# A Winograd form for a 512x1536x512 matmul: seven half-block products in place of eight, in the last two batches and the tails of an attention-and-mixer kernel

## Chip, core and metric

The kernel runs on one core of a Trainium2 chip. The metric is the device time of one execution in microseconds (us). A core has five engines that run side by side: TensorE (PE in the profile; its weight loads are the row PEld), VectorE (DVE), ScalarE (ACT), GpSimd (POOL) and SyncE (SP). SBUF is the on-chip working memory, PSUM the eight banks that matmuls accumulate in.

## What is computed

A linear attention, and behind it an MLP mixer. `x` has 8 batches of 576 rows and 512 columns.

```python
def phi(x, c, s):
    r = np.maximum(x, 0.0)
    return np.concatenate([r * c, r * s], axis=-1)
...
num = np.einsum('bhsf,bhfd->bhsd', q_p, kv)
den = np.einsum('bhsf,bhf->bhs', q_p, z)[..., None] + 1e-06
x = num / den                                     # back as [batch, seq, heads * head_dim]
...
xt = x.transpose(0, 2, 1)
h = np.maximum(xt @ w_tok1, 0.0) @ w_tok2          # token mixing
u = x + h.transpose(0, 2, 1)
h2 = np.maximum(u @ w_ch1, 0.0) @ w_ch2            # channel mixing, 512 -> 1536 -> 512
return u + h2
```

The change touches only the last matmul, `... @ w_ch2`, and the addition of its result to `u`. Inputs and output are float32; the matmul operands are bf16 in the kernel and are summed in float32.

## The kernel before

A batch has 576 = 4 x 128 + 64 rows. The four full blocks of a batch go through one call of `channel`. The left-over 64 rows of all eight batches are gathered, two batches to a block of 128, in `u_tail` (four blocks); one more call of `channel`, the last thing that the kernel does, takes these tails. Batches 0 and 1 are woven by hand into one long list of operations; batches 2 to 7 and the tails go through `channel`:

```python
def channel(uT, u, store, by_slot, hooks, fine=False):
    h1 = one.tile([P, NCH, 4 * P], BF16, name="h1")
    ...
    for mi in range(NCH):                            # NCH = 12: first channel matmul
        c_ps = psM.tile([P, 512], F32, name="c_ps", tag="psM")
        for ki in range(NCC):                        # NCC = 4
            nc.tensor.matmul(c_ps, wc1[:, ki, mi * P:(mi + 1) * P], uT[:, :, ki, :], ...)
        relu(by_slot[mi], h1[:, mi, :], c_ps)        # "A": ScalarE, "D": VectorE
        step()
    for j in range(4):                               # second channel matmul
        if fine and j == 3:
            for cs in (slice(0, Dm // 2), slice(Dm // 2, Dm)):
                o_ps = psM.tile([P, Dm // 2], F32, name="o_ps", tag="psM")
                for ki in range(NCH):
                    nc.tensor.matmul(o_ps, h1[:, ki, j * P:(j + 1) * P], wc2[:, ki, cs], ...)
                nc.vector.tensor_add(u[:, j, cs], o_ps, u[:, j, cs])
                store(j, u, cs)
            break
        o_ps = psM.tile([P, Dm], F32, name="o_ps", tag="psM")
        for half in range(2):
            for ki in range(half * NCH // 2, (half + 1) * NCH // 2):
                nc.tensor.matmul(o_ps, h1[:, ki, j * P:(j + 1) * P], wc2[:, ki, :], ...)
            if half:
                nc.vector.tensor_add(u[:, j, :], o_ps, u[:, j, :])
                store(j, u)
            step()
```

`step()` issues the work of other batches that is hung on the slots of this call: while batch `p` is in `channel`, batch `p+1` goes through its attention and token mixing, and batch `p+2` has its features made. In the call for batch 6 only batch 7 is left to be hung there, in the calls for batch 7 and for the tails nothing is. Parts of batch `p+1` that matter here:

```python
def um(self, g):      # token mixing, two of the four row blocks, into PSUM
    ps = self.psum(("u", g), psA, [P, 2, Dm])
    ...
def uo(self, g):      # VectorE, 1024 elements a partition
    nc.vector.tensor_add(self.sb("u")[:, js, :], self.ps.pop(("u", g)), self.x[:, js, :])
def ubc(self, g, eng="P"):      # GpSimd makes the bf16 copy of u
    copy(eng, self.sb("ub")[:, js, :], self.u[:, js, :])
def utx(self, g):     # transposed by DMA into uT, which the next channel call reads
    nc.sync.dma_start_transpose(...)
```

PSUM is split into `psM` (four one-bank buffers, used in turn) and `psA` (two two-bank buffers). A buffer is written again only after its last reader is done. An engine works through its instructions in the order of the program. Rows go out as soon as they are added up: for a batch after every second `j`, for the tails after every `j`, and in two halves for the last one.

Of the kernel before, what the change touches and what calls it, by code (L numbers as in the profile page):

```python
# [9 lines left out]
F32 = mybir.dt.float32  # L10
BF16 = mybir.dt.bfloat16
AF = mybir.ActivationFunctionType
ALU = mybir.AluOpType

WARM = 20
FIRST = "S"
PLAN = """
feat.0.k.4.2.0.D feat.0.q.0.2.0.A feat.0.q.2.2.1.A feat.0.q.3.2.1.A feat.0.q.4.2.1.D feat.0.q.3.2.0.A
# [40 lines left out]
def kernel(  # L59
# [11 lines left out]
    nc = tc.nc  # L71

    B, H, S, D = q.shape
    Dm = H * D
    _, D_tok = moe_w_tok1.shape
    _, D_ch = moe_w_ch1.shape
    P = 128
    J = S // P
    JA = J + 1
    R = J + JA  # L80
    NP = B // 2
    NCC = Dm // P
    NT = D_tok // P
    NCH = D_ch // P
    HH = H // 2
    VW = D + 2
# [44 lines left out]
    def heads(g):  # L131
        return slice(0, H) if g == 2 else slice(g * HH, (g + 1) * HH)
# [30 lines left out]
    par = const.tile([P, 1], F32, name="par")  # L163
# [36 lines left out]
    for i in range(2):  # L200
        t = const.tile([P, JA, H, VW], BF16, name=f"vbf{i}")
# [7 lines left out]
    w2r = const.tile([P, NT, S], BF16, name="w2r")  # L209
    wc1 = const.tile([P, NCC, D_ch], BF16, name="wc1")  # L210
    wc2 = const.tile([P, NCH, Dm], BF16, name="wc2")
# [44 lines left out]
    u_tail = const.tile([P, NP, Dm], F32, name="u_tail")  # L256
    uT_tail = const.tile([P, NP, NCC, P], BF16, name="uT_tail")
# [8 lines left out]
    def relu(eng, dst, src):  # L266
        if eng == "A":
            nc.scalar.activation(dst, src, AF.Relu)  # L268
        else:
            nc.vector.tensor_relu(dst, src)  # L270

    class Batch:
# [4 lines left out]
        def sb(self, name):  # L277
            if not hasattr(self, name):
                pool, shape, dt = {
                    "kp": (one, [P, JA, H, 2, D], BF16), "qp": (one, [P, JA, H, 2, D], BF16),  # L280
                    "qpT": (two, [P, JA * H, P], BF16), "kv": (two, [P, H, VW], BF16),
                    "x": (two, [P, JA, Dm], BF16), "B1": (two, [P, NT, Dm], BF16),
                    "u": (two, [P, J, Dm], F32), "ub": (one, [P, J, Dm], BF16),
                    "uT": (two, [P, J, NCC, P], BF16), "h1": (one, [P, NCH, 4 * P], BF16)}[name]
                setattr(self, name, pool.tile(shape, dt, name=name))
            return getattr(self, name)
# [248 lines left out]
        def o(self, j):  # L535
            nc.vector.tensor_add(self.u[:, j, :], self.ps.pop(("o", j)), self.u[:, j, :])
            if j % 2:
                for p_ in range(2):
                    nc.sync.dma_start(out=out_rows(self.b, p_, j - 1, 2), in_=self.u[p_::2, j - 1:j + 1, :])
# [36 lines left out]
    def channel(uT, u, store, by_slot, hooks, fine=False):  # L576
        h1 = one.tile([P, NCH, 4 * P], BF16, name="h1")
        slot = 0

        def step():  # L580
            nonlocal slot
            for f in hooks.get(slot, ()):
                f()
            slot += 1

        for mi in range(NCH):
            c_ps = psM.tile([P, 512], F32, name="c_ps", tag="psM")
            for ki in range(NCC):
                nc.tensor.matmul(c_ps, wc1[:, ki, mi * P:(mi + 1) * P], uT[:, :, ki, :],  # L589
                                 start=(ki == 0), stop=(ki == NCC - 1))  # L590
            relu(by_slot[mi], h1[:, mi, :], c_ps)
            step()
        for j in range(4):
# [4 lines that stand above are left out]
                        nc.tensor.matmul(o_ps, h1[:, ki, j * P:(j + 1) * P], wc2[:, ki, cs],  # L598
                                         start=(ki == 0), stop=(ki == NCH - 1))
# [6 lines that stand above are left out]
                    nc.tensor.matmul(o_ps, h1[:, ki, j * P:(j + 1) * P], wc2[:, ki, :],  # L606
                                     start=(ki == 0), stop=(ki == NCH - 1))
                if half:
                    nc.vector.tensor_add(u[:, j, :], o_ps, u[:, j, :])  # L609
                    store(j, u)  # L610
                step()

    def out_rows(b, par, j, n):
        f = JA * par + j if j < J else J
        return out[b].rearrange("(m r) c -> m r c", r=R)[:, f:f + n, :]

    def store_batch(b):
        def store(j, u):
            if j % 2:
                for par in range(2):  # L620
                    nc.sync.dma_start(out=out_rows(b, par, j - 1, 2), in_=u[par::2, j - 1:j + 1, :])
        return store

    def store_tail(j, u, cs=slice(0, Dm)):
        for c, eng in ((0, nc.sync), (1, nc.scalar)):
            eng.dma_start(out=out_rows(2 * j + c, c, J, 1)[:, :, cs], in_=u[c::2, j:j + 1, cs])


    bt = [Batch(b) for b in range(B)]
    OPS = {"ld": ld, "ldp": ldp, "mkid": lambda: make_identity(nc, ident), "wt1": wt1, "wt2": wt2, "wu": wu, "wd": wd, "w2a": w2a}  # L630
    keep_warm(WARM)
    for word in PLAN.split():
        name, *a = word.split(".")
        a = [int(x) if x.isdigit() else x for x in a]
# [5 lines left out]
    def hooks_for(n, m, nxt):  # L640

        h = {}

        def at(slot, f, *a):
            h.setdefault(slot, []).append(lambda: f(*a))
        if nxt is not None:
            at(0, load, nxt, "k")
            at(0, load, nxt, "q")
            if nxt > 5:
                at(9, load, nxt, "v")  # L650
        if n is not None:
            at(0, n.kv_all)
            for j in range(JA):
                at(2 + j, n.num_all, j)
            for j in range(JA):
                at(7 + j // 3, n.mix, j, 2)
            at(8, n.mix_out)
            for g in range(3):
                at(10 + g, n.u_all, g)
        if m is not None:  # L660
            for j in range(JA):
                at(3 + j, m.cast, j, 1, 2, "P")
                at(9 + j, m.q_feature, j)
                at(13 + j, m.k_feature, j)
            at(12, m.turnx, 0, 2)
            at(15, m.turnx, 2, 2)
            at(16, m.turnx, 4, 1)
        if nxt == 5:
            at(16, load, nxt, "v")
        return h  # L670

    evac = ["A"] * 7 + ["D", "A", "D", "D", "D"]
    for p in range(2, B):
        s = bt[p]
        n = bt[p + 1] if p + 1 < B else None
        m = bt[p + 2] if p + 2 < B else None
        nxt = p + 3 if p + 3 < B else None
        channel(s.uT, s.u, store_batch(p), evac if n else ["A", "D"] * 6, hooks_for(n, m, nxt))
    channel(uT_tail, u_tail, store_tail, ["A", "D"] * 6, {}, fine=True)

    _ = tile, bass_utils

# [29 lines left out]
```

## Time and profile before

| what | value |
|---|---|
| time, median of 3 runs | 273.67 us (273.66 to 274.45) |
| span of the profiled execution | 272.8 us |
| TensorE busy | 97% of the span, granted clock 0.999 |
| VectorE / ScalarE / GpSimd busy | 63% / 41% / 17% |
| channel call of batch 6 | 199.75 to 227.34 us |
| channel call of batch 7 | 227.34 to 248.06 us |
| channel call of the tails | 248.06 to 268.85 us |

The times of the calls are read from the chain of work that ended last, where each piece has its start and length. Matmuls are pipelined: the profile lists 379 ns for one of 512 columns, from its start to the modelled end, while one starts every 216 ns. The length of a stretch is therefore read from the chain or from the starts, not from the busy time.

### The profile page before, as it was taken

To read this page: it belongs to the slowest core of one execution; us is meant where nothing else is said; L and a number is where in the kernel's file an instruction comes from. 1 tells how busy PE (TensorE), PEld (TensorE's weight loads), DVE (VectorE), ACT (ScalarE), POOL (GpSimd) and SP (SyncE) were. 2 spreads that over 40 slices of the span, in tenths; PEclk is the share of its full clock that TensorE was granted. 3 is DMA by queue.
4 is the path that set the end of the run, shared out by engine and by line. 5 is a ranking of instruction groups with operands and counts; after the bars stand their busy time and mean duration, and the time that the engine had idled before them with its cause. 6 is when DMAs were issued, how large, how long until landed. Compare 5 with 4: busy or idle time off the path is not lost.

```text
span 272.8 us, 4868 instructions
## 1 busy us (share of the span) xinstructions
PE 263.3 (97%) x1941; PEld 137.9 (51%) x1941; DVE 172.8 (63%) x346; ACT 111.0 (41%) x176; POOL 47.1 (17%) x67
## 2 busy tenths in 40 slices
PE   6988999999999999999999999999999999999994
PEld 2875555456444654455445544654455444444443
DVE  6389788799791658936784679476837643424422
ACT  2886272384491449043904390339133202301300
POOL 2164060040032043002450026002000210000000
PEclk9999999999999999999999999999999999999999
DMA  6999999999999999999999978910980062012012
GB/s 201 359 224 151 249 259 221 366 209 263 370 216 189 322 377 342 211 164 327 363 209 255 313 239 181 211 41 6 218 204 2 0 158 94 0 47 106 2 68 87
DMA packets 79079, 53.37 MB, mean 196 GB/s; under 512 B 47824, under 2 KB 76496, under 8 KB 79056
## 3 DMA queue, kind: packets, MB, share of 16 engines
q1 hardware_dynamic: 74512, 48.77, 66.7%
q0 software_dynamic: 4144, 3.77, 9.3%
q10 hardware_dynamic: 400, 0.52, 0.5%
q8 instruction: 15, 0.25, 0.4%
q14 instruction: 8, 0.07, 0.1%
HBM read 35.85 MB, written 9.44 MB: 166 GB/s over the span
## 4 chain that ended last, share of the span: by engine, by line
PE 82%; DMA 9%; DVE 4%; SPq 1%; issue 1%; POOL 1%; ACT 0%; DVEq 0%
PE c_ps L589 27%; PE o_ps L606 26%; PE o L524 8%; PE b L433 6%; PE u L460 4%; DMA qt<-in_q_dram 4%; PE c L512 4%; PE kv L361 3%; DMA wc<-in_moe_w_ch_dram 3%; PE nf L390 3%; DMA kt<-in_k_dram 2%; SPq L143 1%; DVE kp L332 1%; PE ut L488 1%; PE o_ps L598 1%; DVE h L270 1%
## 5 line engine op out<-in xcount | busy, mean ns | idle before, releaser
L268 ACT ACTIVATE h<-c_ps 128x512 bf16<-128x512 f32 x52 | 31.1, 597 | 107.5 <-PE c_ps L589 64.2
L606 PE MATMUL o_ps<-wc,h 128*128 128x512 bf16 x324 | 71.9, 379 | 0.0
L589 PE MATMUL c_ps<-uT,wc 128*128 128x512 bf16 x288 | 70.4, 379 | 0.0
L606 PEld LDWEIGHTS <-h 128*128 128x128 bf16 x324 | 31.7, 98 | 38.2
L589 PEld LDWEIGHTS <-wc 128*128 128x128 bf16 x336 | 30.8, 98 | 32.6
L270 DVE TENSOR_SCALAR h<-c_ps 128x512 bf16<-128x512 f32 x32 | 22.0, 688 | 28.4 <-PE c_ps L589 28.4
L264 POOL CAST ub<-u 128x1024 bf16<-128x1024 f32 x14 | 15.1, 1083 | 89.5 <-DVE u L465 45.8
L264 POOL CAST vbf<-vt 128x512 bf16<-128x512 f32 (+3 forms) x28 | 18.8, 708 | 65.4 <-DMA vt<-in_v_dram 64.5
L330 ACT ACTIVATE qp<-qt,cos_t 128x512 bf16<-128x512 f32 x33 | 23.1, 712 | 15.6 <-DMA qt<-in_q_dram 13.9
L609 DVE TENSOR_TENSOR u<-o_ps,u 128x512 f32<-128x512 f32 x24 | 16.6, 690 | 18.9 <-PE o_ps L606 18.9
L512 PE MATMUL c<-uT,wc 128*128 128x512 bf16 x96 | 22.7, 379 | 0.0
L524 PE MATMUL o<-wc,h 128*128 128x512 bf16 x96 | 22.0, 379 | 0.0
L413 DVE TENSOR_TENSOR x<-nf,den 128x512 bf16<-128x512 f32 x30 | 20.7, 692 | 1.0
L330 ACT ACTIVATE qp<-qt,sin_t 128x512 bf16<-128x512 f32 x30 | 21.1, 712 | 0.0
L332 DVE TENSOR_SCALAR kp<-kt,cos_t 128x512 bf16<-128x512 f32 x30 | 17.3, 578 | 5.3 <-DMA kt<-in_k_dram 5.3
L465 DVE TENSOR_TENSOR u<-u,x 128x1024 f32<-128x1024 f32 x16 | 19.3, 1220 | 1.7 <-PE u L460 1.5
L390 PEld LDWEIGHTS <-qpT 128*128 128x128 bf16 x320 | 15.2, 98 | 9.9 <-DVE x L413 1.5
L433 PE MATMUL b<-x,w 128*128 128x512 bf16 (+1 forms) x90 | 20.2, 355 | 0.0
L332 DVE TENSOR_SCALAR kp<-kt,sin_t 128x512 bf16<-128x512 f32 x31 | 18.2, 591 | 0.8 <-DMA kt<-in_k_dram 0.8
L460 PE MATMUL u<-B,w 128*128 128x512 bf16 x64 | 16.1, 379 | 0.0
L409 DVE TENSOR_SCALAR den<-nf 128x8 f32<-128x8 f32 x30 | 5.0, 166 | 15.9 <-PE nf L390 15.9
L524 PEld LDWEIGHTS <-h 128*128 128x128 bf16 x96 | 9.1, 98 | 10.2
(92 smaller groups left out, 250.4 us busy)
## 6 DMA issues: line engine op xcount, KB each, us to landing
out_dram<-u SPq DMA_DIRECT2D x32, 256.0 KB, 2.8
qt<-in_q_dram SPq DMA_DIRECT2D x8, 640.0 KB, 8.8
kt<-in_k_dram SPq DMA_DIRECT2D x8, 640.0 KB, 8.3
qt<-in_q_dram SPq DMA_DIRECT2D x8, 512.0 KB, 7.6
kt<-in_k_dram SPq DMA_DIRECT2D x8, 512.0 KB, 7.2
vt<-in_v_dram SPq DMA_DIRECT2D x6, 640.0 KB, 8.3
vt<-in_v_dram SPq DMA_DIRECT2D x6, 512.0 KB, 7.3
wc<-in_moe_w_ch_dram POOLq DMA_DIRECT2D x4, 384.0 KB, 8.2
```

The costliest lines, as they stand in the source:

```text
L264: (nc.scalar.copy if eng == "A" else ENG[eng].tensor_copy)(dst, src)
L268: nc.scalar.activation(dst, src, AF.Relu)
L270: nc.vector.tensor_relu(dst, src)
L330: nc.scalar.activation(dst, src, AF.Relu, scale=tab)
L332: ENG[eng].tensor_scalar(dst, src, scalar1=tab, scalar2=0.0, op0=ALU.mult, op1=ALU.max)
L390: nc.tensor.matmul(nm[:, hh * (D + 1):(hh + 1) * (D + 1)], self.qpT[:, j * H + h, :], self.kv[:, h, :D + 1], start=(not eps or hh == 0), s ...
L433: nc.tensor.matmul(b1[:, mi], w1[:, col(self.c, j), mi * P:(mi + 1) * P], self.x[:, j, cs], start=(j == 0 and (g == 2 or mi == 0)), stop=( ...
L460: nc.tensor.matmul(ps[:, jj], w2[:, ki, 1 + 2 * g + jj, :], self.B1[:, ki, :], start=(ki == 0), stop=(ki == NT - 1))
L512: nc.tensor.matmul(ps, wc1[:, ki, mi * P:(mi + 1) * P], self.uT[:, :, ki, :], start=(ki == 0), stop=(ki == NCC - 1))
L524: nc.tensor.matmul(self.ps["o", j], self.h1[:, ki, j * P:(j + 1) * P], wc2[:, ki, :], start=(ki == 0), stop=(ki == NCH - 1))
L589: nc.tensor.matmul(c_ps, wc1[:, ki, mi * P:(mi + 1) * P], uT[:, :, ki, :], start=(ki == 0), stop=(ki == NCC - 1))
L606: nc.tensor.matmul(o_ps, h1[:, ki, j * P:(j + 1) * P], wc2[:, ki, :], start=(ki == 0), stop=(ki == NCH - 1))
```

## The change

The second channel matmul multiplies a 512 x 1536 matrix (rows `a`) by a 1536 x 512 matrix (`wc2`). Both are cut into 2 x 2 blocks: `a` into blocks of 256 x 768, `wc2` into blocks of 768 x 256. The ordinary way needs eight block products. Winograd's form of Strassen's method needs seven, and in exchange sums of blocks: four combined blocks of rows for each call (`s1`, `s2`, a new `a21`, and later a new `s2`), and four combined blocks of weights (`t1` to `t4`), made once, in the call of batch 6. The results are recombined when they are added to `u`. The form is used where `p >= QUADS = 6` and for the tails. `t1` is written over a quarter of `wc2`, so every call from then on has to use the new form.

To make room in SBUF for `t2` to `t4`, `s1`, `s2`, `vb` and `vc`, the tiles `qpT` and `x` go from two buffers to one, and `va` lies over `w2r`, which is no longer needed then.

```diff
-                    "qpT": (two, [P, JA * H, P], BF16), "kv": (two, [P, H, VW], BF16),
-                    "x": (two, [P, JA, Dm], BF16), "B1": (two, [P, NT, Dm], BF16),
+                    "qpT": (one, [P, JA * H, P], BF16), "kv": (two, [P, H, VW], BF16),
+                    "x": (one, [P, JA, Dm], BF16), "B1": (two, [P, NT, Dm], BF16),
...
+        return [lambda: nc.vector.tensor_sub(t3, quad(1, 1), quad(0, 1)),
+                lambda: nc.vector.tensor_sub(t1, quad(0, 1), quad(0, 0)),
+                lambda: nc.gpsimd.tensor_sub(t2, quad(1, 1), t1),
+                lambda: nc.vector.tensor_sub(t4, quad(1, 0), t2)]
+
+    def channel7(uT, u, store, by_slot, hooks, fine=False):
...
+        def s_part(dst, f, a, b, n):
+            ks = (slice(0, 4), slice(4, K2))[n]
+            f(dst[:, ks], a[:, ks], b[:, ks])
+
+        def product(ps, a, b, first, jjs=(0, 1)):
+            for jj in jjs:
+                for ki in range(K2):
+                    nc.tensor.matmul(ps[jj] if isinstance(ps, list) else ps[:, jj], a[:, ki, jj * P:(jj + 1) * P], b[:, ki],
...
+            relu(by_slot[mi], h1[:, mi, :], c_ps)
+            if mi == NCH - 2:
+                s_part(s1, nc.vector.tensor_add, a21, a22, 0)
+                s_part(s2, nc.vector.tensor_sub, s1, a11, 0)
+            if mi == NCH - 1:
+                s_part(s1, nc.vector.tensor_add, a21, a22, 1)
+                s_part(s2, nc.vector.tensor_sub, s1, a11, 1)
+            step()
+        Dk = bank()
+        if fine:
+            A = [bank()[:, 0], psA.tile([P, D2], F32, name="m2_ps", tag="psA")]
...
+        else:
+            A = bank()
+            product(A, a11, quad(0, 0), True)
+            nc.scalar.copy(va, A)
+        nc.vector.tensor_sub(a21, a11, a21)
+        step()
+        product(Dk, a22, t4, True)
+        nc.scalar.copy(vb, Dk)
+        nc.gpsimd.tensor_sub(u22, u22, vb)
+        step()
+        Bk = bank()
+        product(Bk, s2, t2, True)
+        nc.vector.tensor_add(va, Bk, va)
+        nc.vector.tensor_sub(s2, a12, s2)
+        step()
+        C = bank()
+        product(C, s1, t1, True)
+        nc.scalar.copy(vc, C)
+        nc.gpsimd.tensor_add(u12, u12, va)
+        nc.gpsimd.tensor_add(u22, u22, vc)
+        step()
+        product(Dk, a21, t3, False)
+        nc.vector.tensor_add(vb, Dk, va)
+        wide = bass.AP(tensor=vb.tensor, offset=vb.offset, ap=[vb.ap[0], [D2, 2], [0, 2], [1, D2]])
+        u2 = u[:, 2:4, :].rearrange("p j (a d) -> p j a d", a=2)
+        nc.vector.tensor_add(u2, u2, wide)
+        store(2, u, 2)
+        step()
+        product(C, s2, quad(1, 1), False)
+        nc.vector.tensor_add(u12, C, u12)
+        step()
+        if fine:
+            store(0, u, 2, slice(D2, Dm))
+            for jj in range(2):
+                product(A, a12, quad(1, 0), False, (jj,))
+                nc.vector.tensor_add(u11[:, jj], A[jj], u11[:, jj])
+            store(0, u, 2, slice(0, D2))
+        else:
+            product(A, a12, quad(1, 0), False)
+            nc.vector.tensor_add(u11, A, u11)
+            store(0, u, 2)
...
+            at(18, n.u_all, 2)                                  # call of batch 6: slot 12 before
...
+            for f, slot in zip(quad_weights(), (0, 0, 0, 8)):   # in the call of batch 6
...
+    evac7 = ["A"] * 7 + ["D", "A", "D", "D", "A"]
+    evac2 = ["A"] * 4 + ["D", "A"] * 4
...
+        if p < QUADS:
+            channel(s.uT, s.u, store_batch(p), evac, hooks_for(n, m, nxt))
+        else:
+            channel7(s.uT, s.u, store_batch(p), evac7 if n else evac2, hooks7(n, m, nxt, p == QUADS))
+    channel7(uT_tail, u_tail, store_tail, evac2, {}, fine=True)
```

The rows of blocks 2 and 3 now go out together, and then those of blocks 0 and 1; for the tails the latter in two halves of the columns.

More of the change, by code (lines that the diff above doesn't have):

```diff
@@ L15 @@
 WARM = 20
+QUADS = 6
 FIRST = "S"
@@ L611, in channel, with quad, quad_weights @@
                 step()
+    K2, D2 = NCH // 2, Dm // 2
+    t2, t3, t4 = (const.tile([P, K2, D2], BF16, name=f"t{i}") for i in (2, 3, 4))
+    def quad(a, b):
+        return wc2[:, a * K2:(a + 1) * K2, b * D2:(b + 1) * D2]
+    t1 = quad(0, 1)
+    def quad_weights():
+        return [lambda: nc.vector.tensor_sub(t3, quad(1, 1), quad(0, 1)),
+                lambda: nc.vector.tensor_sub(t1, quad(0, 1), quad(0, 0)),
+                lambda: nc.gpsimd.tensor_sub(t2, quad(1, 1), t1),
+                lambda: nc.vector.tensor_sub(t4, quad(1, 0), t2)]
@@ new lines, in channel7, with step, tok, bank @@
+    def channel7(uT, u, store, by_slot, hooks, fine=False):
+        h1 = one.tile([P, NCH, 4 * P], BF16, name="h1")
+        slot = 0
+        def step():
+            nonlocal slot
+            for f in hooks.get(slot, ()):
+                f()
+            slot += 1
+        def tok(a, b):
+            return h1[:, a * K2:(a + 1) * K2, b * 2 * P:(b + 1) * 2 * P]
+        a11, a12, a21, a22 = tok(0, 0), tok(1, 0), tok(0, 1), tok(1, 1)
+        s1 = one.tile([P, K2, 2 * P], BF16, name="s1")
+        s2 = one.tile([P, K2, 2 * P], BF16, name="s2")
+        va = w2r.rearrange("p n s -> p (n s)").bitcast(F32)[:, :2 * D2].rearrange("p (a b) -> p a b", a=2)
+        vb = one.tile([P, 2, D2], F32, name="vb")
+        vc = one.tile([P, 2, D2], F32, name="vc")
+        u11, u12 = u[:, 0:2, :D2], u[:, 0:2, D2:]
+        u21, u22 = u[:, 2:4, :D2], u[:, 2:4, D2:]
+        def s_part(dst, f, a, b, n):
[5 more added lines that the diff above has]
+                    nc.tensor.matmul(ps[jj] if isinstance(ps, list) else ps[:, jj], a[:, ki, jj * P:(jj + 1) * P], b[:, ki],
+                                     start=(first and ki == 0 and (jj == 0 or isinstance(ps, list))), stop=ki == K2 - 1,
+                                     skip_group_check=True)
+        def bank():
+            return psM.tile([P, 2, D2], F32, name="m_ps", tag="psM")
+        for mi in range(NCH):
+            c_ps = psM.tile([P, 512], F32, name="c_ps", tag="psM")
+            for ki in range(NCC):
+                nc.tensor.matmul(c_ps, wc1[:, ki, mi * P:(mi + 1) * P], uT[:, :, ki, :],
+                                 start=(ki == 0), stop=(ki == NCC - 1))
+            relu(by_slot[mi], h1[:, mi, :], c_ps)
[10 more added lines that the diff above has]
+            for jj in range(2):
+                product(A, a11, quad(0, 0), True, (jj,))
+                nc.scalar.copy(va[:, jj], A[jj])
+        else:
[31 more added lines that the diff above has]
+            store(0, u, 2, slice(D2, Dm))
+            for jj in range(2):
+                product(A, a12, quad(1, 0), False, (jj,))
[5 more added lines that the diff above has]
+            store(0, u, 2)
+        step()
+        step()
@@ L617, in store_batch, with store, store_tail @@
     def store_batch(b):
[L618 to L621, printed above, removed]
-        return store
-    def store_tail(j, u, cs=slice(0, Dm)):
+        def store(j, u, n=1, cs=None):
+            if n == 1 and j % 2 == 0:
+                return
+            j -= j % 2
+            for par in range(2):
+                nc.sync.dma_start(out=out_rows(b, par, j, 2), in_=u[par::2, j:j + 2, :])
+        return store
+    def store_tail(j, u, n=1, cs=slice(0, Dm)):
+        rows = out.rearrange("b (m r) c -> m r b c", r=R)[:, J]
         for c, eng in ((0, nc.sync), (1, nc.scalar)):
-            eng.dma_start(out=out_rows(2 * j + c, c, J, 1)[:, :, cs], in_=u[c::2, j:j + 1, cs])
+            eng.dma_start(out=rows[:, 2 * j + c:2 * (j + n):2, cs], in_=u[c::2, j:j + n, cs])
     bt = [Batch(b) for b in range(B)]
@@ L670, in hooks_for, with hooks7, at @@
         return h
+    def hooks7(n, m, nxt, quads):
+        h = {}
+        def at(slot, f, *a):
+            h.setdefault(slot, []).append(lambda: f(*a))
+        if nxt is not None:
+            at(0, load, nxt, "k")
+            at(0, load, nxt, "q")
+            at(16 if nxt == 5 else 9, load, nxt, "v")
+        if n is not None:
+            at(0, n.kv_all)
+            for j in range(JA):
+                at(2 + j, n.num_all, j)
+            for j in range(JA):
+                at(7 + j // 3, n.mix, j, 2)
+            at(8, n.mix_out)
+            at(10, n.u_all, 0)
+            at(11, n.u_all, 1)
+            at(18, n.u_all, 2)
+        if m is not None:
+            for j in range(JA):
+                at(3 + j, m.cast, j, 1, 2, "P")
+            for i, slot in enumerate((1, 2, 3, 4, 5, 6, 9, 10, 11, 12)):
+                at(slot, m.feat, "q", i // 2, 2, i % 2, "A")
+            for i, slot in enumerate((7, 7, 7, 8, 8, 9, 13, 14, 15, 16)):
+                at(slot, m.feat, "k", i // 2, 2, i % 2, "D" if i < 6 else "A")
+            at(12, m.turnx, 0, 2)
+            at(14, m.turnx, 2, 2)
+            at(15, m.turnx, 4, 1)
+        if quads:
+            for f, slot in zip(quad_weights(), (0, 0, 0, 8)):
+                at(slot, f)
+        return h
     evac = ["A"] * 7 + ["D", "A", "D", "D", "D"]
+    evac7 = ["A"] * 7 + ["D", "A", "D", "D", "A"]
+    evac2 = ["A"] * 4 + ["D", "A"] * 4
     for p in range(2, B):
@@ L677 @@
         nxt = p + 3 if p + 3 < B else None
-        channel(s.uT, s.u, store_batch(p), evac if n else ["A", "D"] * 6, hooks_for(n, m, nxt))
-    channel(uT_tail, u_tail, store_tail, ["A", "D"] * 6, {}, fine=True)
+        if p < QUADS:
[3 more added lines that the diff above has]
+    channel7(uT_tail, u_tail, store_tail, evac2, {}, fine=True)
     _ = tile, bass_utils
```

## The prediction

> **What bounds the kernel now.** I read the page first: busy shares, then the granted clock in the 40 slices.
>
> ```profile
> PE 263.3 (97%) x1941; PEld 137.9 (51%) x1941; DVE 172.8 (63%) x346; ACT 111.0 (41%) x176; POOL 47.1 (17%) x67
> ...
> PEclk9999999999999999999999999999999999999999
> ```
>
> TensorE is busy nearly throughout, at full clock. Busy time alone proves little, so next comes the chain of work that ended last, here the end of the list (start, length, what):
>
> ```profile
> 227.34 10.36 PE c_ps L589 x48
> 237.70 10.36 PE o_ps L606 x48
> 248.06 10.36 PE c_ps L589 x48
> 258.42 7.77 PE o_ps L606 x36
> 266.19 2.63 PE o_ps L598 x24
> 268.85 0.42 DVE u_tail L600
> ```
>
> Here the three affected stretches lie matmul behind matmul, no other engine between them: TensorE sets the time. 10.36/48 = 216 ns for a matmul of 512 columns. L598 already runs matmuls of 256 columns, each with its own weight load: 2.63/24 = 110 ns. So the half blocks of the change should not pay for their more frequent weight loads. After the last addition (269.27) come 3.5 us to the end of the span: the last store and the close.
>
> Then the stretches of batch 6, batch 7, tail products and end, for what else is busy (length, then PE, PEld, DVE, ACT, POOL, clock, DMA share, GB/s):
>
> ```profile
> 199.75:227.34 27.59, 27.59 (x198) 13.91 (x196) 14.30 (x27) 6.40 (x10) 2.70 (x3) 1.00 0.31 79
> 227.34:248.06 20.72, 20.72 (x97) 9.37 (x96) 6.92 (x10) 3.58 (x6) 0.00 (x0) 1.00 0.13 51
> ```
>
> VectorE is half idle in batch 6 and two thirds idle in batch 7; GpSimd has three casts in the first and nothing in the second. That is room on average; the order in time decides. The durations that I use are from the groups by form:
>
> ```profile
> L465 DVE TENSOR_TENSOR u<-u,x 128x1024 f32<-128x1024 f32 x16 | 19.3, 1220 | 1.7 <-PE u L460 1.5 <-DMA kt<-in_k_dram 0.2
> L264 POOL CAST ub<-u 128x1024 bf16<-128x1024 f32 x14 | 15.1, 1083 | 89.5 <-DVE u L465 45.8 <-issue 43.5
> L609 DVE TENSOR_TENSOR u<-o_ps,u 128x512 f32<-128x512 f32 x24 | 16.6, 690 | 18.9 <-PE o_ps L606 18.9
> ```
>
> Last, do VectorE and GpSimd disturb each other? The timeline around 140 us: first VectorE alone, then with GpSimd beside it, then GpSimd's line.
>
> ```profile
> 138.32 0.48 DVE L332 TENSOR_SCALAR kp<-kt,cos_t 128x512 bf16<-128x512 f32 x1
> ...
> 140.64 0.83 DVE L332 TENSOR_SCALAR kp<-kt,sin_t 128x512 bf16<-128x512 f32 x1
> 141.39 0.83 DVE L332 TENSOR_SCALAR kp<-kt,cos_t 128x512 bf16<-128x512 f32 x1
> ```
> ```profile
> 139.82 3.61 POOL L264 CAST vbf<-vt 128x512 bf16<-128x512 f32 x5 [3.66 <-DMA vt<-in_v_dram]
> ```
>
> The same VectorE operation goes from 0.48 to 0.83 us while GpSimd casts, and five casts take 3.61 us here against 2.85 at 127.63. They take turns.
>
> **What the skill says.** (1) The Trainium skill, "TensorE: Matmul & The Clock Gate", section "Wait — 56ns, not 53.3ns?": a warm matmul starts every N / 2.4 GHz + about 2.5 ns, 109 ns for 256 columns. The trace agrees (110). (2) "VectorE: DVE Perf Modes", "The perf-mode tier table": an operation on two bf16 tensors in SBUF runs two elements a cycle, float32 one. For float32 the page's (N+151)/0.96 gives 691 ns at 512, and the trace has 690. For bf16 it makes, as estimates, 424, 690 and 957 ns at 512, 1024 and 1536 elements; no such operation is in this trace. (3) "GPSIMD Engine Reference", "3.1 Elementwise — side-by-side cycle accounting": a GpSimd addition of 2048 float32 takes 4497 ns. The trace has no two-input GpSimd operation; its casts (median 1042 ns at 1024 elements, 616 at 512) show a fixed part of 190. Scaling the rest gives an estimate of 1.27 us at 512. (4) "SBUF — State Buffer", "Who interferes with whom": a VectorE operation with both inputs in SBUF and a GpSimd operation that reads SBUF exclude each other. The trace shows turns for VectorE's one-input operation (above), not for two inputs.
>
> **The change part by part.**
>
> *TensorE.* A call has 7 products x 12 = 84 matmuls of 256 columns: 84 x 110 = 9.2 us. Removed: 10.36 us each for batches 6 and 7, 7.77 + 2.63 = 10.40 for the tails. Saved if nothing waits: 1.16 + 1.16 + 1.20 = 3.5 us. Only an eighth of the product goes, and these calls are three of nine: even the ideal is 1.3% of 273.67.
>
> *Buffers.* `x` and `qpT` with one buffer: in a call the last readers (additions of slots 10 to 12, numerators of slots 2 to 6) precede the next writer (slot 2, slot 12). In the first third the first DMA transpose into `qpT` is at 54.45, the last numerator of the batch before it starts at 50.0. No cost.
>
> *Weights.* Two VectorE operations of 0.96 us at the start of batch 6, where VectorE idles 3.42 us before the first `den` (203.91); `t2` on GpSimd (estimate 3.4 us) and `t4` about nine slots later. Beside other work: 0.
>
> *Row sums before the third product.* `s1`, `s2` need 0.69 + 0.69 us after the eleventh block and 0.42 + 0.42 after the last ReLU, that is about 2.3 us after the first product's start (time 0 from here). The third product starts at 2 x 1.31 = 2.63. They just fit: 0.
>
> *The closing chain.* This is the part that I doubt. Products of 1.31 us end at 1.31 ... 9.20; a result is readable some 0.2 us later. Batch 7: `vb` is copied at 3.45. GpSimd: `u22 -= vb` 3.45 to 4.7. At 4.85 `va` is ready, and two operations start on it at once, GpSimd's `u12 += va` and VectorE's 0.96 us `s2` update, both reading SBUF. If they exclude each other with VectorE first, GpSimd starts at 5.8, ends `u12` at 7.0 and `u22 += vc` at 8.2. Only then can VectorE add the wide 1024 elements (1.22, to 9.4), then `u12` (to 10.05), then `u11` (to 10.7). The bank of `A` is free at 10.7, and the second block of the next call wants it at 9.20 + 0.86 = 10.06: TensorE waits 0.65. Net for batch 7: -1.16 + 0.65 = -0.5. In batch 6 two casts of 1.04 us and two additions of 1.22 for batch 7 stand in the same queues; the chain ends about 1.2 later (11.9), TensorE wants the bank at 9.20 + 0.43 + 0.86 = 10.5: wait 1.4, net about +0.2.
>
> *The tails' end.* Before, the last addition ended 269.27 - 258.26 = 11.0 us after the first product's start. Now it is the same chain, 10.7: -0.3. But 1 MB of output, until now spread from 261.8 on, goes out in the last 1.4 us of it. A pair of 256 KB stores takes 2.8 us to land, the last small ones before took 2; I give back 0.3. Net 0.
>
> Sum with exclusion: -0.5 + 0.2 + 0 = -0.3. Without it (`u22` done 7.35 in batch 7, 7.85 in batch 6) the waits vanish, the tails' last addition comes at about 10.2 instead of 10.7: -1.1 - 1.1 - 0.6 = -2.8. I weigh exclusion in full or part at 0.6: 0.6 x (-0.3) + 0.4 x (-2.8) = -1.3, so 272.4 us.
>
> **Rivals.** *A, all of TensorE's saving arrives*: 270.2. For it: the rate of 110 ns is measured, VectorE has idle time. Against: in-order queues, and the tails end in additions and stores. *B, the closing chain on GpSimd and VectorE becomes the bound* and TensorE waits for the bank: 273.4, the case worked out above; the turns at 140 us speak for it. If two-input GpSimd work is slower than 1.27 us, each 0.1 us costs 0.3 us per call, and the change loses: up to 274.5. *C, bf16 operations run one element a cycle* (strided blocks): `s1`, `s2` end at about 3.2, the third product waits 0.6, the sixth another 0.5 to 1.4: some 1.5 us a call, 275 to 277. Against: the rows inside a block are contiguous. *D, the stores at the end are the bound*: the end comes up to 0.8 us later.
>
> **Range and chances.** A bounds the gain, so 270.6 is the low end; B with slow GpSimd or D give the high end, 274.4. Over 2% faster would be under 268.2, more than the removed matmuls hold: 0.02. Over 2% slower is above 279.1, beyond C: 0.03.
>
> **What would show it.** Right: L606 and L598 lose their batch 6, 7 and tail matmuls, 252 of 256 columns come at 110 ns; no new wait before 200 us; the wait list gains TensorE's first channel matmul on VectorE, in the second block after each of the two batches, 0.5 to 1.5 us. GpSimd's additions show 1.1 to 1.4 us alone, more beside VectorE. Wrong: the chain unbroken matmuls over both borders (then A); waits inside the products, before the third or sixth (then C); bf16 sums of 1024 elements at 1.2 us rather than 0.7; or the last store landing over 3 us after its issue (D).

## The result, and the profile after

| kernel | time (median) | ratio to before | 95% interval |
|---|---|---|---|
| before | 273.67 us | 1 | |
| changed | 272.16 us | 0.9939 | 0.9914 to 0.9964 |
| changed, once more beside e9 | 272.23 us | 0.9943 | 0.9929 to 0.9957 |

About 1.5 us or 0.6% less; 272.4 had been predicted. First the busy shares of the changed kernel, then its chain of work that ended last, from the first product of batch 6 on (start, length, what; `u_tail` L701 is GpSimd's `u12 += va`, L712 and L718 are VectorE's last additions). `POOLq` and `DVEq` are time that the chain spends in an engine's queue, `issue` is time for which it names no wait; by the engines' own timelines GpSimd's `u22 += vc` (262.00 to 263.26) and VectorE's wide addition (263.30 to 264.53) fall in the stretches listed as `POOLq` and `issue`.

```profile
PE 260.1 (96%) x2037; PEld 147.4 (54%) x2037; DVE 185.7 (69%) x365; ACT 119.3 (44%) x191; POOL 64.3 (24%) x77
```
```profile
215.70 9.17 PE m_ps L657 x84
224.87 0.43 PE ut L489 x2
225.30 10.49 PE c_ps L667 x48
235.79 9.17 PE m_ps L657 x84
244.96 10.36 PE c_ps L667 x48
255.32 3.94 PE m_ps L657 x36
...
260.13 1.16 POOL u_tail L701
261.36 1.92 POOLq L863
263.33 1.11 issue
264.44 0.68 DVE u_tail L712
265.12 0.33 DVEq L863
265.45 0.33 DVE u_tail L718
```

Each set of 84 matmuls takes 9.17 us (109 ns apiece) where 10.36 stood. At the border behind batch 6 the 48 matmuls take 10.49 instead of 10.36: the only new wait in this stretch, 0.13 us. Behind batch 7 there is none. In the tails the chain leaves TensorE halfway through the products and ends on GpSimd and VectorE, which it did not before.

The start of batch 6's call lies at 199.75 in the profile before and at 198.90 in the one after. These 0.85 us arise in the first third, where the chain starts with the arrival of loads: from the first call of `channel` (89.42 before, 88.57 after) to that of batch 6 both take 110.33 us. I leave them out, and measure the tails from the start of their own first product matmul to the end of the span:

| from the tails' first product | before | changed |
|---|---|---|
| TensorE's products done | 10.6 us | 9.3 us |
| last addition ends | 11.0 | 10.6 |
| end of the span | 14.54 | 15.34 |

The sum is then -1.19 (batch 6) + 0.13 - 1.19 (batch 7) + 0.80 (tails) = -1.45 us, against -1.51 measured. The question that is left: why do two calls keep everything and one lose more than it gained?

### The profile page after: what moved, and what is told of

Its sections match the earlier page's. It is cut to its first block, busy times and chain, and to the rows that moved or that the text cites. A ratio compares the mean times of both kernels' runs of the same rounds, so it can differ in the third digit from the quotient of the medians.

```text
span 270.5 us, 5124 instructions
## 1 busy us (share of the span) xinstructions
PE 260.1 (96%) x2037; PEld 147.4 (54%) x2037; DVE 185.7 (69%) x365; ACT 119.3 (44%) x191; POOL 64.3 (24%) x77
## 4 chain that ended last, share of the span: by engine, by line
PE 81%; DMA 9%; DVE 3%; SPq 1%; POOL 1%; issue 1%; POOLq 1%; DVEq 0%; ACT 0%
PE o_ps L607 15%; PE c_ps L590 15%; PE c_ps L667 12%; PE m_ps L657 8%; PE o L525 8%; PE b L434 6%; PE c L513 5%; PE u L461 4%; DMA qt<-in_q_dram 4%; PE kv L362 3%; DMA wc<-in_moe_w_ch_dram 3%; PE nf L391 3%; DMA kt<-in_k_dram 2%; PE ut L489 1%; SPq L144 1%; DVE kp L333 1%
## 5 line engine op out<-in xcount | busy, mean ns | idle before, releaser
L269 ACT ACTIVATE h<-c_ps 128x512 bf16<-128x512 f32 x57 | 34.0, 597 | 92.1 <-issue 43.6
L607 PE MATMUL o_ps<-wc,h 128*128 128x512 bf16 x192 | 42.7, 379 | 0.0
L271 DVE TENSOR_SCALAR h<-c_ps 128x512 bf16<-128x512 f32 x27 | 18.6, 688 | 25.4 <-PE c_ps L590 12.8
L607 PEld LDWEIGHTS <-h 128*128 128x128 bf16 x192 | 18.8, 98 | 22.7
L667 PEld LDWEIGHTS <-wc 128*128 128x128 bf16 x144 | 13.7, 98 | 15.5 <-issue 0.3
L333 DVE TENSOR_SCALAR kp<-kt,sin_t 128x512 bf16<-128x512 f32 x31 | 17.5, 569 | 1.3 <-DMA kt<-in_k_dram 1.3
L657 PEld LDWEIGHTS <-h 128*128 128x128 bf16 x144 | 14.1, 98 | 2.3
```

Source lines behind the costliest of these rows:

```text
L333: ENG[eng].tensor_scalar(dst, src, scalar1=tab, scalar2=0.0, op0=ALU.mult, op1=ALU.max)
L657: nc.tensor.matmul(ps[jj] if isinstance(ps, list) else ps[:, jj], a[:, ki, jj * P:(jj + 1) * P], b[:, ki], start=(first and ki == 0 and (j ...
```

## Experiments

All are edits of the changed kernel; times are medians, and "tail" is the stretch from the tails' first product to the end of the span in the run's own profile.

| run | time, us | ratio to before (95% interval) | tail, us |
|---|---|---|---|
| e1 batches only | 271.47 | 0.9926 (0.9901 to 0.9951) | 14.51 |
| e2 tails only | 274.50 | 1.0025 (1.0015 to 1.0035) | 15.31 |
| e3 banks, edit without effect | 272.23 | 0.9944 (0.9923 to 0.9965) | 15.31 |
| e4 a tail store left out | 271.98 | 0.9933 (0.9912 to 0.9953) | 14.70 |
| e5 bank of A second | 274.18 | 1.0016 (1.0004 to 1.0027) | 15.37 |
| e6 tails reordered | 271.89 | 0.9934 (0.9913 to 0.9954) | 14.92 |
| e7 tail additions on VectorE | 271.41 | 0.9913 (0.9895 to 0.9931) | 14.74 |
| e8 update before sum | 274.5, one run | none | 15.94 |
| e9 tails reordered again | 271.36 | 0.9913 (0.9899 to 0.9927) | 14.64 |
| e10 changed kernel again | 272.23 | 0.9943 (0.9929 to 0.9957) | 15.35 |
| e11 and whole rows | 270.81 | 0.9904 (0.9887 to 0.9921) | 14.26 |
| e12 and one addition on GpSimd | 271.38 | 0.9923 (0.9906 to 0.9941) | 14.64 |

### e1 and e2: each part alone

```diff
# both: `channel` takes the changed `store`, and t1 lies in memory of its own (that of a k tile no longer needed), so wc2 stays whole
-                    store(j, u, cs)
+                    store(j, u, 1, cs)
...
-    t1 = quad(0, 1)
+    t1 = raw["k", 0].rearrange("p h c -> p (h c)").bitcast(BF16)[:, :K2 * D2].rearrange("p (k d) -> p k d", k=K2)
# e1
-    channel7(uT_tail, u_tail, store_tail, evac2, {}, fine=True)
+    channel(uT_tail, u_tail, store_tail, ["A", "D"] * 6, {}, fine=True)
# e2
-            channel7(s.uT, s.u, store_batch(p), evac7 if n else evac2, hooks7(n, m, nxt, p == QUADS))
+            channel(s.uT, s.u, store_batch(p), evac if n else ["A", "D"] * 6, hooks7(n, m, nxt, p == QUADS))
```

> Seven products in the calls of batches 6 and 7, the ordinary eight for the tails (t1 gets memory of its own, so that wc2 stays whole). Theory T (both batch calls keep TensorE's full saving of 1.19 us, less a wait of 0.13; the tails' call loses 0.8 by its end): the loss goes away, 273.67 - 2 x 1.19 + 0.13 = 271.4 us, 0.8 under the changed kernel. Rival R (every call gains about the same third of 1.5 us): 273.67 - 1.0 = 272.7. End after the last addition: 3.5 us under T.

> The other way round: seven products for the tails alone, the ordinary form in batches 6 and 7, the combined weights still made in the call of batch 6. Theory T: TensorE ends 1.2 us earlier and the end comes 2.0 later than that: 273.67 + 0.8 = 274.5 us. Rival R (every call gains a third): 273.2.

Measured: 271.47 and 274.50. Both are theory T to within 0.1 us. In e1's profile the end comes 3.5 us after the last addition, as T said. The new form in the two batches is worth 2.2 us; in the tails it costs 0.8, and alone makes the kernel slower, with an interval (1.0015 to 1.0035) clear of 1.

### e3 and e5: why TensorE did not wait at the borders

My prediction had the second block of the next call wait for the bank of `A`, the last that the closing chain frees. In e3 I meant to bring that about by taking four banks ahead and using them in another order.

```diff
+        ahead = [psM.tile([P, 512], F32, name="c_ps", tag="psM") for _ in range(4)] if turn else None
...
+            if turn and mi < 4:
+                c_ps = ahead[(1, 3, 0, 2)[mi]]
```

> The changed kernel, but the first four blocks of the calls for batch 7 and for the tails take their PSUM banks in the turn that the prediction assumed: Dk, A, Bk, C, in place of Bk, Dk, C, A. Theory T (the predicted waits did not come only because the bank of A is wanted last): TensorE waits about 1.6 us in the second block of batch 7 (A free 12.05 after the first product, wanted 10.46) and 0.6 in that of the tails (10.6 against 10.03), in all about 2.0 us more: 274.2. Rival R (the bank's order does not matter, TensorE has slack elsewhere): 272.2.

Measured: 272.23. That is R's number, but no test of it: in the program as built, the blocks had kept the banks of `Bk`, `Dk`, `C`, `A`, exactly as without the edit, because a bank is given at the first use, and the one freed first in the order of the program is given first. The buffers of `psM` are thus not used in turn, as I had written further up. The traces agree: VectorE's `u12` addition (L712) is the last reader of `C`, its `u11` addition (L722) that of `A`. In the changed kernel, behind batch 6:

```profile
226.26 0.68 DVE L712 TENSOR_TENSOR u<-m_ps,u 128x512 f32<-128x512 f32 x1
226.86 0.68 DVE L722 TENSOR_TENSOR u<-m_ps,u 128x512 f32<-128x512 f32 x1
```

The third block starts at 227.00, 0.13 us late and just after `u12` is done (226.95); in e3 it is 227.33 after 227.27. So the 0.13 us are a wait for the bank of `C`. The fourth block starts at 227.86, and `A` is free at 227.54, with 0.3 us to spare. To test what its order is worth, e5 uses the very tile of `A` for the second block.

```diff
+            if mi == 1 and last_a:
+                c_ps = last_a.pop().rearrange("p a b -> p (a b)")
+            else:
                 c_ps = psM.tile([P, 512], F32, name="c_ps", tag="psM")
...
             nc.vector.tensor_add(u11, A, u11)
+            last_a.append(A)
```

> The changed kernel, but the second block of the calls for batch 7 and for the tails is summed in the very bank of A that the call before leaves (the banks then come in the order Bk, A, Dk, C). Theory T (the predicted waits did not come only because the bank of A is wanted fourth): TensorE waits about 1.6 us in the second block of batch 7 (A free 12.05 us after the first product, wanted at 10.46) and 0.6 in that of the tails (10.6 against 10.03), where there was 0.13 before: about 2.0 us more than the changed kernel, 274.2. Rival R (the order of the banks does not matter): 272.2.

Measured: 274.18, and the waits where theory T put them, each some 0.2 us shorter than it said. TensorE's timeline of e5 (start, length, operation; in brackets its idle time before and who ended it):

```profile
227.32 1.02 PE L672 MATMUL m_ps<-uT,wc 128*128 128x512 bf16 x4 [1.44 <-DVE u L727]
...
247.43 1.02 PE L672 MATMUL m_ps<-uT_tail,wc 128*128 128x512 bf16 x4 [0.43 <-DVE u L727]
```

1.4 and 0.4 us of waiting for the `u11` addition (L727 here): the closing chain is about as late as predicted, and only the turn of the banks kept it from TensorE. In the changed kernel the bank of `A` is wanted by the fourth block, 1.73 us later than by the second.

### e8: do GpSimd and VectorE exclude each other?

In the changed kernel GpSimd's three additions of 512 float32 in batch 7 look like this, with the VectorE operation that begins beside the second (start, length):

```profile
239.11 1.26 POOL L691 TENSOR_TENSOR u<-u,vb 128x512 f32<-128x512 f32 x1 [9.57 <-ACT vb L690]
240.60 1.91 POOL L701 TENSOR_TENSOR u<-u,w2r 128x512 f32<-128x512 f32 x1 [0.22 <-DVE w2r L695]
242.48 1.26 POOL L702 TENSOR_TENSOR u<-u,vc 128x512 f32<-128x512 f32 x1
```
```profile
240.44 0.95 DVE L696 TENSOR_TENSOR s<-h,s 128x1536 bf16<-128x1536 bf16 x1
```

The second takes 0.65 us longer. It is also the one that reads `va`, which lies over `w2r` (hence that name), so its place could be the reason.

```diff
-        nc.vector.tensor_add(va, Bk, va)
         nc.vector.tensor_sub(s2, a12, s2)
+        nc.vector.tensor_add(va, Bk, va)
```

> The changed kernel with the order of two VectorE operations turned round after the third product: the s2 update (two bf16 inputs in SBUF) before the sum with va, so that GpSimd's u12 += va, which needs that sum, no longer runs beside it. Theory T (the two exclude each other): u12 += va takes 1.26 us like the other two GpSimd additions, but starts about 0.9 later, and the time stays the same. Rival R (this addition is slower in itself, through the place that va lies in): it stays at 1.9 us and the whole comes 0.6 us or more later.

The same operations in e8:

```profile
240.71 1.26 POOL L691 TENSOR_TENSOR u<-u,vb 128x512 f32<-128x512 f32 x1 [9.57 <-ACT vb L690]
243.47 1.27 POOL L701 TENSOR_TENSOR u<-u,w2r 128x512 f32<-128x512 f32 x1 [1.49 <-DVE w2r L696]
```
```profile
241.36 1.43 DVE L695 TENSOR_TENSOR s<-h,s 128x1536 bf16<-128x1536 bf16 x1 [1.11 <-PE m_ps L657]
```

With nothing beside it, the addition that reads `va` takes 1.27 us: its place does not matter. Now VectorE's update runs beside GpSimd's first addition and is the one held up (1.43 instead of 0.95). So whichever of the two comes second is delayed; in e6 and e12 below a float32 addition of VectorE that starts beside one of GpSimd's takes 1.04 us instead of 0.68. On the time I was wrong: I had overlooked that the update would run into the first addition, and the tail grew by 0.6 us. The 274.5 of this single run holds another 1.6 us of late loads (batch 6's first product at 217.13 instead of 215.53), so I draw nothing from it.

### e4 and e7: what the tails lose at their end

The windows of the changed kernel after the tails' products (length, then busy PE, PEld, DVE, ACT, POOL, granted clock, DMA share, where 1 is all 16 DMA engines busy, GB/s):

```profile
266.00:267.00 1.00, 0.00 (x0) 0.00 (x0) 0.00 (x0) 0.00 (x0) 0.00 (x0) 1.00 1.03 383
267.00:268.00 1.00, 0.00 (x0) 0.00 (x0) 0.00 (x0) 0.00 (x0) 0.00 (x0) 1.00 0.99 342
268.00:269.00 1.00, 0.00 (x0) 0.00 (x0) 0.00 (x0) 0.00 (x0) 0.00 (x0) 1.00 0.80 273
```

The 16 DMA engines are full, or nearly so, for 3 us with the 1 MB that goes out at once, and after 265.8 us no engine computes any more. e4 leaves half of it out:

```diff
         nc.vector.tensor_add(u2, u2, wide)
-        store(2, u, 2)
+        if not fine:
+            store(2, u, 2)
```

> The changed kernel without the store of blocks 2 and 3 of the tails (512 KB of the output are left out; all else is computed). Theory T (the end is bound by 1 MB going out in one burst after 264.5 us): the last stores land about 2.4 us after their issue instead of 3.1 and wait for nothing before them, 1.0 to 1.2 us less: 271.0 to 271.2. Rival R (the end is the chain of additions and a fixed landing time): 272.1 to 272.2.

Measured: 271.98, just 0.2 under the changed kernel, well within both intervals, and nearer to R than to T. The tail in its profile is 0.64 us shorter (14.70); in the five profiles whose tails are those of the changed kernel (the changed kernel, e2, e3, e5, e10) it is 15.31 to 15.37, so this difference is clear. The landing of the last stores did fall as expected, the last transfers of the kernel before first (KB each, us to landing), then those of the changed kernel and of e4:

```profile
out_dram<-u_tail ACTq DMA_DIRECT2D x2, 64.0 KB, 2.1
```
```profile
out_dram<-u_tail ACTq DMA_DIRECT2D x2, 128.0 KB, 3.1
```
```profile
out_dram<-u_tail ACTq DMA_DIRECT2D x2, 128.0 KB, 2.5
```

Leaving the store out also takes its issues out of the two queues, and the last issue starts at 10.8 us after the first product instead of 11.05. So the burst, with its issues, is part of the loss, about 0.6 us by the profile, and not the 1.0 to 1.2 that T gave it. An issue costs its queue time, here those of the kernel before, with one row block each, and of the changed kernel, with two (ns min/median/max, first and last start):

```profile
L626 ACTq DMA_DIRECT2D out_dram<-u_tail x5: 502/504/557, 261.8 to 269.3; - x5
```
```profile
L743 ACTq DMA_DIRECT2D out_dram<-u_tail x3: 633/727/739, 264.6 to 266.2; - x3
```

The additions ahead of the stores are taken up by e7:

```diff
-        nc.gpsimd.tensor_sub(u22, u22, vb)
+        adder = nc.vector if fine else nc.gpsimd
+        adder.tensor_sub(u22, u22, vb)
...
-        nc.gpsimd.tensor_add(u12, u12, va)
-        nc.gpsimd.tensor_add(u22, u22, vc)
+        adder.tensor_add(u12, u12, va)
+        adder.tensor_add(u22, u22, vc)
```

> The changed kernel with the tails' three GpSimd additions done by VectorE in the same places of the program. Theory T (GpSimd's additions, one of them held up by VectorE, are what the wide addition waits for): the wide addition starts 7.7 us after the first product instead of 8.1, the last one ends at 10.1 instead of 10.6, the stores go out as much earlier: 0.5 us less, 271.6. Rival R (VectorE is then itself too full, or the end is bound by the stores alone): 272.0 to 272.5.

Measured: 271.41 (T: 271.6). VectorE's timeline of the changed kernel, then of e7; their tails begin at the same 255.16, so the starts compare directly:

```profile
263.30 1.23 DVE L708 TENSOR_TENSOR u_tail<-u_tail,vb 128x1024 f32<-128x1024 f32 x1 [0.64 <-POOL u_tail L702]
264.44 0.68 DVE L712 TENSOR_TENSOR u_tail<-m_ps,u_tail 128x512 f32<-128x512 f32 x1
265.04 0.75 DVE L718 TENSOR_TENSOR u_tail<-m_ps,u_tail 128x256 f32<-128x256 f32 x2
```
```profile
262.69 1.23 DVE L709 TENSOR_TENSOR u_tail<-u_tail,vb 128x1024 f32<-128x1024 f32 x1
263.83 0.68 DVE L713 TENSOR_TENSOR u_tail<-m_ps,u_tail 128x512 f32<-128x512 f32 x1
264.43 0.74 DVE L719 TENSOR_TENSOR u_tail<-m_ps,u_tail 128x256 f32<-128x256 f32 x2
```

The 0.64 us that VectorE waited for GpSimd is gone, and the end comes 0.6 earlier. Even with three more additions VectorE is done sooner than with GpSimd's help.

### e6, e9, e11, e12: a better end for the tails

If the additions and the late stores are the loss, a different order of the products should help: `A`, `Dk`, `Bk`, `Dk2`, `C`, `A2`, `C2`, with each part of the rows stored when it is ready.

```diff
# e6, in the fine case; pb holds C in two banks
+            product(Dk, a21, t3, False)
+            nc.vector.tensor_add(vb, Dk, va)
+            nc.vector.tensor_add(u21, u21, vb)
+            store(2, u, 2, slice(0, D2))
+            nc.vector.tensor_add(u22, u22, vb)
+            for jj in range(2):
+                product(pb, s1, t1, True, (jj,))
+                nc.scalar.copy(vc[:, jj], pb[jj])
+            nc.vector.tensor_add(u22, u22, vc)
+            store(2, u, 2, slice(D2, Dm))
+            product(A, a12, quad(1, 0), False)
+            nc.vector.tensor_add(u11, A, u11)
+            store(0, u, 2, slice(0, D2))
+            for jj in range(2):
+                product(pb, s2, quad(1, 1), False, (jj,))
+                nc.vector.tensor_add(u12[:, jj], pb[jj], u12[:, jj])
+            store(0, u, 2, slice(D2, Dm))
```

> The changed kernel with the tails' call put in another order: products A, Dk, Bk, Dk2, C, A2, C2, each quarter of u_tail stored as soon as it is added up (four stores of 256 KB instead of one of 512 and two of 256), two of the three GpSimd additions replaced by VectorE ones. Theory T (the tails lose at the end because the additions queue up behind GpSimd and 1 MB then goes out at once): the last addition ends 9.8 to 10.0 us after the first product instead of 10.6, the end comes 3.5 to 3.9 after it instead of 4.7: 1.5 to 1.8 us less than the changed kernel, 270.4 to 270.7. Rival R (the end costs the same in any order, being the landing of 1 MB after TensorE is done): 271.8 to 272.2.

Measured: 271.89, which is R's range. Of the three GpSimd additions the edit moved only one to VectorE, `u22 += vc`. Why so little was won shows in ScalarE's and TensorE's timelines:

```profile
263.77 0.65 ACT L698 COPY vc<-m_ps 128x256 f32<-128x256 f32 x2 [4.88 <-DVE u_tail L695]
```
```profile
264.19 1.47 PE L657 MATMUL m_ps<-wc,s 128*128 128x256 bf16 x12 [0.69 <-ACT vc L698]
```

Half of the stores are issued from ScalarE's queue, and mine stood ahead of the copies of `C`: they waited behind a store that waited for VectorE, and TensorE waited 0.69 us for the copies. Of the 4.88 us that ScalarE was idle, 2.74 also stand in e9, where it waits for the product itself; the store cost the other 2.1. e9 puts the copies first, gives all additions to VectorE and halves the last store:

```diff
# against e6
-            store(2, u, 2, slice(0, D2))
             nc.vector.tensor_add(u22, u22, vb)
             for jj in range(2):
                 product(pb, s1, t1, True, (jj,))
                 nc.scalar.copy(vc[:, jj], pb[jj])
+            store(2, u, 2, slice(0, D2))
...
-            store(0, u, 2, slice(D2, Dm))
+                store(jj, u, 1, slice(D2, Dm))
```

> The tails' call reordered as in the earlier try (products A, Dk, Bk, Dk2, C, A2, C2, each quarter stored when it is ready), but all additions on VectorE, ScalarE's copies of C ahead of its first store in its queue, and the last quarter stored in two halves by row block. Theory T (what the tails lose at the end is the queue of additions and the late burst of stores): no wait of TensorE inside the products, the last addition ends about 10.0 us after the first product, the last store lands sooner; the end comes 13.6 to 14.0 us after the first product (changed kernel 15.3, kernel before 14.5): 1.3 to 1.7 us less than the changed kernel, 270.5 to 270.9. Rival R (the end of the tails cannot get below that of the ordinary form, 14.5): 271.3 or more.

> The changed kernel once more on the same chip, to have its time beside that of the reordered tails: 272.2 by both theories, 0.55% under the kernel before.

Measured: 271.36 beside 272.23 for the changed kernel. The wait of TensorE is gone, and 0.9 us are won, not 1.3 to 1.7, which is R's range again: the tail is 14.64, no better than the ordinary form's 14.5. The last addition ends at 10.3 us, but the queues issue one store behind another:

```profile
262.10 4.78 ACTq L775 DMA_DIRECT2D out_dram<-u_tail  x5
```

Five stores at 0.55 to 0.80 us each; the last begins at 266.3, almost 1 us after the last addition (265.33). e11 stores whole rows, in three pairs:

```diff
# against e9
-            store(2, u, 2, slice(0, D2))
             nc.vector.tensor_add(u22, u22, vc)
-            store(2, u, 2, slice(D2, Dm))
+            store(2, u, 2)
...
             nc.vector.tensor_add(u11, A, u11)
-            store(0, u, 2, slice(0, D2))
...
-                store(jj, u, 1, slice(D2, Dm))
+                store(jj, u)
```

> The reordered tails, stored in three pairs of whole rows (blocks 2 and 3 together as soon as both halves are added up, then block 0, then block 1) instead of five pairs of half rows. Theory T (in the reordered tails the last store is late because five issues of 0.55 to 0.8 us stand behind one another in each queue): the last issue starts within 0.1 us of the last addition (10.3 us after the first product) instead of 0.9, the end comes 13.7 to 14.1 us after the first product instead of 14.6: 0.5 to 0.9 less than the reordered tails, 270.5 to 270.9. Rival R (the end is the landing of what is stored late, however it is issued): 271.3 to 271.6.

Measured: 270.81, tail 14.26 (T: 13.7 to 14.1), ratio 0.9904: the lowest median of all, though its interval overlaps those of e7, e9 and e12. The last issue starts at 265.9, 0.3 us after the last addition (265.62). e12 takes one addition from VectorE:

```diff
# against e11
+            nc.gpsimd.tensor_add(u12, u12, va)
             product(Dk, a21, t3, False)
...
-            nc.vector.tensor_add(u12, u12, va)
             nc.vector.tensor_add(u11, A, u11)
```

> As the whole-row tails, with u12 += va given to GpSimd right after va is there, since VectorE works without a pause up to its last addition. Theory T (VectorE's queue of additions sets the last addition): 0.6 us less work for VectorE, some 0.35 of it given back where GpSimd holds up an addition of two SBUF tensors, so the last addition ends at about 10.0 instead of 10.3 and the time is 0.2 to 0.3 under the whole-row tails. Rival R (exclusion takes all of it, or more): the same or up to 0.4 more.

Measured: 271.38, which is more than even R gave by the medians (0.6 over e11), and within it by the tails (14.64 against 14.26). The last addition does end at 10.0 us, as T said. But the first store, half of all the bytes, starts at 8.8 us after the first product instead of 8.4, because VectorE's addition ahead of it is held up by GpSimd (1.04 us instead of 0.69). The three stores now follow one another faster and take longer to land. e11 first, then e12:

```profile
out_dram<-u_tail ACTq DMA_DIRECT2D x2, 128.0 KB, 2.4
```
```profile
out_dram<-u_tail ACTq DMA_DIRECT2D x2, 128.0 KB, 2.9
```

Here an earlier last addition was worth nothing, with the stores before it later and still under way. That the full DMA engines are the reason is my reading of e4 and e12 together, and not shown: no run changed the spacing of the stores alone.

## Why the prediction was right, and where it was not

The time was 0.24 us off, but my middle came from weighing two outcomes, 273.4 and 270.9, and neither happened. The exclusion that I gave 0.6 did come, and with it my sum was 273.4. Taking off the 1.92 us of waits that did not come, and adding the 0.8 us that the tails lost, makes 272.25, against 272.16 measured. Two errors of opposite sign left the time between my two outcomes, about where the weighing had put the middle; that it came so close is luck.

- **TensorE's rate**: right. 109 ns a matmul, 1.19 us a call (1.16 given).
- **Buffers and weights at no cost**: right. From the first call of `channel` to that of batch 6 both kernels take 110.33 us, and from there to batch 6's first product, with the weights made in between, both take 16.80 (199.75 to 216.55 before, 198.90 to 215.70 after). `t2` took 3.09 us on GpSimd (estimate 3.4), in time for its use.
- **Row sums fit before the third product**: right, in batch 6 by 0.36 us: there the last sum stood beside a GpSimd cast, took 1.14 us instead of 0.42 and ended at 217.80, ahead of the third product at 218.16. The groups of the changed kernel show the bf16 sums at the rates worked out from the Trainium skill, "VectorE: DVE Perf Modes", section "The perf-mode tier table" (424, 690 and 957 ns):

```profile
L687 DVE TENSOR_TENSOR h<-h 128x1536 bf16<-128x1536 bf16 x3 | 2.8, 949 | 0.0
L652 DVE TENSOR_TENSOR s<-h 128x1024 bf16<-128x1024 bf16 x3 | 2.0, 682 | 0.0
L652 DVE TENSOR_TENSOR s<-h 128x512 bf16<-128x512 bf16 x3 | 1.3, 418 | 0.0
```

- **The closing chain in time**: right, step by step. In batch 7, from the first product (235.63): `u22` done at 8.1 (8.2 given), wide addition done at 9.4 (9.4), `u11` at 10.6 (10.7); in batch 6 `u11` at 12.0 (11.9). A lone GpSimd addition takes 1.26 us (1.27 given), and the exclusion that the skill states in "SBUF — State Buffer", section "Who interferes with whom" is there for two SBUF inputs: 1.26 becomes 1.91 in one order, 0.95 becomes 1.43 in the other (e8).
- **"The second block of the next call wants it"**: the failed step for the batches. I took the four banks in turn. They are given in the order in which they were freed, so `A` comes fourth, and TensorE never waited for it: given 0.65 us behind batch 7 and 1.4 behind batch 6, found 0 and 0; the 0.13 behind batch 6 was for the bank of `C`. e5 restores the assumption and gets 0.4 and 1.4 back, 274.18 in all.
- **"I give back 0.3 ... Net 0"**: the failed step for the tails. The last addition came as given (10.6), but from there to the end it took 4.7 us instead of 3.5, that is 1.2 given back. I had reckoned with a somewhat longer landing alone. In the profile the last of three issues starts 0.4 us after its data is ready (0.03 before), because an issue of two row blocks takes 0.63 to 0.74 us where one row block took 0.47 to 0.56, and it lands in 3.1 us instead of 2.1 (128 KB each where 64 stood). Leaving out 512 KB takes 0.6 of the 1.2 away (e4); what is left there is an issue 0.2 us late and a landing of 2.5. That the bytes alone lengthen the landing is not shown.
- **Rivals**: A was right for the batches. D was right in size for the tails (0.8 us later, a landing of over 3 us), but the stores are not the bound alone: taking the additions off GpSimd moves the end by 0.6 us too (e7). B was right in its chain and wrong in its effect; C did not occur. My range began at 270.6, above A's own 270.2, and so left A out.

## What to carry to other kernels

A form that saves matmuls pays where another call follows and hides its recombination, and can lose where nothing follows: look at the last use separately. Ahead of a claim that a buffer makes an engine wait, find out which buffer comes next, and in what order they are freed. At the end of a kernel count the stores too: how many bytes leave at once, how many issues stand in one queue, and what else waits behind them in it.

## What the runs showed beyond that

- An engine that also issues stores passes their waits on: ScalarE's copies came 2.1 us late in e6, behind a store that waited for VectorE.
- Of the 3.6 us that seven products take off TensorE in three calls (3 x 1.19), the changed kernel delivers 1.5. With the ordinary tails (e1) 2.2 arrive, with the reordered whole-row tails (e11) 2.7, from 273.49 to 270.81 on the same chip.
